# A cached-attention block on one core: new row sizes for K and V, one load queue, P as the weights of P*V, projection by token groups

## The chip, the cores and the metric

The kernel runs on one core of one Trainium2 chip. The time is the device time of one execution in microseconds. The profile is of one execution, and its span goes from the first to the last instruction.

## The reference

32 sequences (B) with 4 new tokens each attend to 2048 cached keys. There are 32 query heads in 4 groups (Hkv) of 8, a head has 128 columns, and all is bf16.

```python
q = (x @ wq).reshape(B, Sq, Hq, Dh).transpose(0, 2, 1, 3)      # x [32,4,1024], wq [1024,4096]
k = jnp.repeat(k_cache, rep, axis=1)                           # k_cache, v_cache [32,4,2048,128]
scores = jnp.einsum("bhqd,bhkd->bhqk", q, k) * (Dh ** -0.5)
p = softmax(scores, axis=-1)
o = jnp.einsum("bhqk,bhkd->bhqd", p, v)                        # v repeated like k
return o.transpose(0, 2, 1, 3).reshape(B, Sq, Hq * Dh) @ wo    # wo [4096,1024]
```

K and V are 67.1 MB each, wq and wo 8.4 MB each. One sequence ("a batch" below) has 2.1 MB of K and 2.1 MB of V, and its 32 heads by 4 tokens fill the 128 partitions of a score matrix of 128 by 2048, 32 partitions to a group.

## The kernel before

All instructions are written out by hand for each engine, with semaphores between them. The order on an engine is the order in the text.

- **Loads.** SP's queue has x, then wq in four parts of 1024 columns (line 278, rows of 2 KB), then K of batches 2 to 31, each as four loads of 512 KB, one for a group (line 283, rows of 4 KB); ACT's queue has K of batches 0 and 1 (L516). POOL's queue has V, one load of 2 MB per batch with rows of 4 KB (L268), and wo in 32 loads of 256 KB, one behind each V from batch 2 on (L260). K has two buffers, V three. K of batch b waits until K of b-2 has been transposed, V of b until P*V of b-3 is done.
- **K transposed.** PE turns K, 128 keys at a time, into a ring of four PSUM banks, eight transposes to a bank (a "fill", L312). DVE copies five of the eight fills of a batch to `KT_sb` (L444), ACT three (L446). This runs two batches ahead.
- **Scores.** 16 matmuls (L397) with the queries of one group as weights (32 columns) and 512 keys streaming, in four column tiles of PE, write `ps_s`, four banks. DVE takes the maximum over 2048 (L481) and scales it (L484), ACT takes the exponential with the row sum (L539) into `P_sb`.
- **P transposed and normalised.** DVE makes the reciprocal of the sum (L493) and a diagonal matrix of it (`diag`, L498). 16 matmuls of P with diag (L328) give the normalised transposed P in f32, four fills of the same ring; DVE and ACT copy two each to `PT_sb` (L444, L446).
- **P*V.** 64 matmuls (L346): a block of V, 128 by 128, is the weights and 32 columns of transposed P stream. The result is O transposed; DVE copies it to `oT_sb` (L453).
- **Projection.** After the last batch 64 matmuls of 512 columns (L418) with `oT_sb` as weights give the output for all 128 tokens; DVE and ACT copy a half each (L509, L556), and SP stores it (L286).

PE's order for batch i is QK of i, P*V of i-1, the fills of K of i+2, the transposes of P of i:

```python
for c in range(Sk // 512):
    for g in range(G):
        ins = eng.matmul(ps_s[32*g:32*(g+1), c*512:(c+1)*512], ...)   # QK of i
mark_ev("pe", ins, f"qk{i}")
if i >= 1:
    do_pv(i - 1)
if i + KT_AHEAD < B:
    do_kt_fills(i + KT_AHEAD)
do_tr_fills(i)
```

Of the kernel before, what the change touches and what calls it, by code (L numbers as in the profile page):

```python
# [12 lines left out]
class _Counter:  # L13

    def __init__(self, sem):
        self.sem = sem
        self.n = 0

    def mark(self, ins):
        self.n += 1  # L20
        ins.then_inc(self.sem, 1)
        return self.n


def bass_standalone__gqa_block_cached__sampling_kernel(
# [9 lines left out]
    _, Hkv, Sk, Dh = k_cache.shape  # L35
    Hq = wq.shape[1] // Dh
    REP = Hq // Hkv
    NT = B * Sq
    assert NT == 128 and Dh == 128 and Hkv * REP * Sq == 128 and D % 128 == 0
    assert Sk == 2048 and wo.shape[0] == Hq * Dh and wo.shape[1] == D and D == 1024  # L40
    KT = D // 128
    NKT = Sk // 128
    G = Hkv
    scale = float(Dh) ** -0.5
# [3 lines left out]
    NRING = 4  # L48
    KT_FILLS = 2 * G
    TR_FILLS = 4  # L50
    WQC = 1024
    NWQC = (Hq * Dh) // WQC
    HPC = WQC // Dh

# [3 lines left out]
    def kt_consumer(f):  # L58
        return "act" if f in (4, 6, 7) else "dve"

    def tr_consumer(f):
        return "dve" if f in (0, 2) else "act"

    jobs = []

    def add_kt(b):
        for f in range(KT_FILLS):
            jobs.append(("kt", b, f, kt_consumer(f)))

    def add_tr(b):  # L70
        for f in range(TR_FILLS):
            jobs.append(("tr", b, f, tr_consumer(f)))

    KT_AHEAD = 2
    for b in range(KT_AHEAD):
        add_kt(b)
    for i in range(B):
        if i + KT_AHEAD < B:
            add_kt(i + KT_AHEAD)
        add_tr(i)  # L80
    job_index = {(k, b, f): j for j, (k, b, f, c) in enumerate(jobs)}
    def last_pv_before_job(j):
        kind, b, f, _ = jobs[j]
        if kind == "kt":
            return b - KT_AHEAD - 1
        else:
            return b - 1

    ev = {}

    def plan():
        cnt = {"pe": 0, "dve": 0, "act": 0, "pool": 0}

        def mark(e, name):
            cnt[e] += 1
            assert name not in ev, name
            ev[name] = (e, cnt[e])

        mark("pool", "ident")
        mark("pe", "xT")  # L100
        for f in range(KT_FILLS):
            mark("pe", ("fill", job_index[("kt", 0, f)]))
        for j in range(Hq // 8):
            mark("pe", f"qproj_bank{j}")
        for f in range(KT_FILLS):
            mark("pe", ("fill", job_index[("kt", 1, f)]))
        for j in range(Hq // 8, Hq // 4):
            mark("pe", f"qproj_bank{j}")
        for i in range(B):
            mark("pe", f"qk{i}")  # L110
            if i >= 1:
                mark("pe", f"pv{i - 1}")
            if i + KT_AHEAD < B:
                for f in range(KT_FILLS):
                    mark("pe", ("fill", job_index[("kt", i + KT_AHEAD, f)]))
            for f in range(TR_FILLS):
                mark("pe", ("fill", job_index[("tr", i, f)]))
        mark("pe", f"pv{B - 1}")
        for c in range(2):
            mark("pe", f"oproj{c}")  # L120
        mark("dve", "xT_evac")
        for f in range(KT_FILLS):
            if kt_consumer(f) == "dve":
                mark("dve", ("evac", job_index[("kt", 0, f)]))
        for j in range(0, Hq // 8, 2):
            mark("dve", f"q_evac{j}")
        for f in range(KT_FILLS):
            if kt_consumer(f) == "dve":
                mark("dve", ("evac", job_index[("kt", 1, f)]))
        for j in range(Hq // 8, Hq // 4, 2):  # L130
            mark("dve", f"q_evac{j}")
        for i in range(B):
            mark("dve", f"max{i}")
            mark("dve", f"negmax{i}")
            if i >= 1:
                mark("dve", f"ot_evac{i - 1}")
            if i + KT_AHEAD < B:
                for f in (0, 1, 2):
                    if kt_consumer(f) == "dve":
                        mark("dve", ("evac", job_index[("kt", i + KT_AHEAD, f)]))  # L140
            mark("dve", f"rinv{i}")
            mark("dve", f"diag{i}")
            if i + KT_AHEAD < B:
                for f in range(3, KT_FILLS):
                    if kt_consumer(f) == "dve":
                        mark("dve", ("evac", job_index[("kt", i + KT_AHEAD, f)]))
            for f in range(TR_FILLS):
                if tr_consumer(f) == "dve":
                    mark("dve", ("evac", job_index[("tr", i, f)]))
        mark("dve", f"ot_evac{B - 1}")  # L150
        mark("dve", "out_evac0")
        for f in range(KT_FILLS):
            if kt_consumer(f) == "act":
                mark("act", ("evac", job_index[("kt", 0, f)]))
        for j in range(1, Hq // 8, 2):
            mark("act", f"q_evac{j}")
        for f in range(KT_FILLS):
            if kt_consumer(f) == "act":
                mark("act", ("evac", job_index[("kt", 1, f)]))
        for j in range(Hq // 8 + 1, Hq // 4, 2):  # L160
            mark("act", f"q_evac{j}")
        for i in range(B):
            mark("act", f"exp{i}")
            if i + KT_AHEAD < B:
                for f in range(KT_FILLS):
                    if kt_consumer(f) == "act":
                        mark("act", ("evac", job_index[("kt", i + KT_AHEAD, f)]))
            for f in range(TR_FILLS):
                if tr_consumer(f) == "act":
                    mark("act", ("evac", job_index[("tr", i, f)]))  # L170
        mark("act", "out_evac1")

    plan()

    with ExitStack() as es:
        w_sb = es.enter_context(nc.sbuf_tensor("w_sb", [128, KT, Hq * Dh], BF16))
        wq_sb = w_sb
        wo_view = w_sb[:, :, :].rearrange("p a (c n) -> p (a c) n", n=D)
        K_sb = es.enter_context(nc.sbuf_tensor("K_sb", [128, NKB, G, NKT * Dh], BF16))
        V_sb = es.enter_context(nc.sbuf_tensor("V_sb", [128, NVB, G, NKT * Dh], BF16))  # L180
        KT_sb = es.enter_context(nc.sbuf_tensor("KT_sb", [128, NKTB, G, Sk], BF16))
        QT_sb = es.enter_context(nc.sbuf_tensor("QT_sb", [128, B, Hq, Sq], BF16))
        oT_sb = es.enter_context(nc.sbuf_tensor("oT_sb", [128, Hq, NT], BF16))
        pp_sb = es.enter_context(nc.sbuf_tensor("pp_sb", [128, 2, Sk], BF16))
        P_sb = pp_sb[:, 0, :]
        PT_sb = pp_sb[:, 1, :].rearrange("p (t r) -> p t r", r=128)
        x_sb = pp_sb[:, 0, 0:D]
        xT_sb = pp_sb[:, 0, D:2 * D].rearrange("p (a b) -> p a b", b=128)
        out_sb = pp_sb[:, 1, 0:D]
        ident = es.enter_context(nc.sbuf_tensor("ident", [128, 128], BF16))  # L190
        diag = es.enter_context(nc.sbuf_tensor("diag", [128, 2, 128], BF16))
        mx = es.enter_context(nc.sbuf_tensor("mx", [128, B], F32))
        negmx = es.enter_context(nc.sbuf_tensor("negmx", [128, B], F32))
        ssum = es.enter_context(nc.sbuf_tensor("ssum", [128, B], F32))
        rinv = es.enter_context(nc.sbuf_tensor("rinv", [128, B], F32))

        ps_s = es.enter_context(nc.psum_tensor("ps_s", [128, Sk], F32))
        ps_a = es.enter_context(nc.psum_tensor("ps_a", [128, 512], F32))
        ps_b = es.enter_context(nc.psum_tensor("ps_b", [128, 512], F32))
        ps_c = es.enter_context(nc.psum_tensor("ps_c", [128, 512], F32))  # L200
        ps_o = es.enter_context(nc.psum_tensor("ps_o", [128, 512], F32))
        ring_f32 = [ps_a[:, :], ps_b[:, :], ps_c[:, :], ps_o[:, :]]
        ring_bf16 = [p.bitcast(BF16) for p in ring_f32]
        ps_x = ring_bf16[2]

        s_x = es.enter_context(nc.semaphore("s_x"))
        s_wq = [es.enter_context(nc.semaphore(f"s_wq{i}")) for i in range(NWQC)]
        s_wo = es.enter_context(nc.semaphore("s_wo"))
        s_out = es.enter_context(nc.semaphore("s_out"))
        s_k = [[es.enter_context(nc.semaphore(f"s_k{i}_{g}")) for g in range(G)] for i in range(NKB)]  # L210
        s_v = [es.enter_context(nc.semaphore(f"s_v{i}")) for i in range(NVB)]
# [376 lines left out]
```

## Time and profile before

| | us |
|---|---|
| the two runs shown | 411.44 and 409.82 |
| their median | 410.63 |
| span of the profiled execution (the page gives no other time of it) | 409.6 |
| PE, DVE, ACT busy | 306.7 (75%), 244.7 (60%), 197.2 (48%) |
| moved by DMA | 152.33 MB, mean 372 GB/s |

The page has the busy time of each engine, then the span in 40 slices of 10.2 us: a digit is the busy share in tenths, and GB/s is what the DMA engines moved. A group of instructions is shown with its line, engine, operation, the tile written and read, the count, busy time, mean duration in ns, idle time before it and what ended that. In the timeline the first column is the start, the second the duration. A row of waits has the total, the number of times and the longest.

### The profile page before, as it was taken

How to read it: one execution, taken by the hardware profiler on the slowest of the kernel's cores; microseconds unless marked ns; L12 is line 12 of the kernel's file. 1: busy time of each engine (PE TensorE's matmuls, PEld its weight loads, DVE VectorE, ACT ScalarE, POOL GpSimd, SP SyncE). 2: the span in 40 equal slices, each digit the busy share in tenths (PEclk: the TensorE clock that was granted, in tenths of full speed). 3: DMA queues.
4: the chain of work that ended last, by engine and by line, in shares of the span. 5: the costliest groups of instructions: out<-in, count | busy, mean ns of one | idle time of the engine just before them, and what ended most of it. 6: DMA issues, size and time to landing. Idle time of an engine off the chain costs nothing.

```text
span 409.6 us, 12650 instructions
## 1 busy us (share of the span) xinstructions
PE 306.7 (75%) x5448; PEld 251.4 (61%) x5448; DVE 244.7 (60%) x390; ACT 197.2 (48%) x230; POOL 42.0 (10%) x70
## 2 busy tenths in 40 slices
PE   4576877988777687577777777759876787775596
PEld 4476766867655576466666566548765676674442
DVE  2113286786666587677766776745875867765400
ACT  1213066474555555555555455553555555545300
POOL 0001011110100111111111111110110111120000
PEclk9799799998999899999999999997998989889679
DMA  8999999999999999999999999999999999997000
GB/s 307 400 387 401 408 408 407 407 406 407 407 407 408 405 406 407 406 407 407 408 404 407 407 407 406 407 407 406 407 406 407 407 407 408 403 402 308 38 2 26
DMA packets 42390, 152.33 MB, mean 372 GB/s; under 512 B 3168, under 2 KB 3168, under 8 KB 42336
## 3 DMA queue, kind: packets, MB, share of 16 engines
q0 software_dynamic: 19456, 75.50, 46.3%
q1 hardware_dynamic: 21728, 71.84, 44.7%
q10 hardware_dynamic: 1152, 4.19, 2.6%
q8 instruction: 44, 0.72, 0.7%
q14 instruction: 10, 0.08, 0.1%
HBM read 151.26 MB, written 0.26 MB: 370 GB/s over the span
## 4 chain that ended last, share of the span: by engine, by line
DMA 53%; PE 28%; issue 6%; SPq 5%; DVE 4%; ACT 3%; ACTq 0%; DVEq 0%
DMA K_sb<-in_k_cache_dram 32%; DMA V_sb<-in_v_cache_dram 15%; DMA w_sb<-in_wq_dram 6%; PE ps_o L346 5%; PE ps_s L418 4%; PE ps_o L312 4%; PE ps_s L397 3%; SPq L278 3%; PE ps_c L312 3%; PE ps_a L312 3%; PE ps_b L312 2%; SPq L283 2%; ACT KT_sb L446 2%; DVE mx L481 2%; PE ps_s L371 2%
## 5 line engine op out<-in xcount | busy, mean ns | idle before, releaser
L539 ACT ACTIVATE pp_sb<-ps_s,negmx 128x2048 bf16<-128x2048 f32 x32 | 62.9, 1967 | 98.7 <-DVE negmx L484 98.7
L481 DVE TENSOR_REDUCE mx<-ps_s 128x1 f32<-128x2048 f32 x32 | 73.3, 2292 | 43.8 <-PE ps_s L397 43.8
L346 PEld LDWEIGHTS ps_o<-pp_sb,V_sb 128*128 128x128 bf16 x2048 | 53.9, 96 | 25.9 <-issue 16.6
L346 PE MATMUL ps_o<-pp_sb,V_sb 128*128 128x32 bf16 x2048 | 57.4, 178 | 11.5 <-DMA V_sb<-in_v_cache_dram 7.0
L312 PE MATMUL ps_c<-ident,K_sb 128*128 128x128 bf16 x512 | 43.6, 232 | 19.7 <-DMA K_sb<-in_k_cache_dram 15.1
L268 POOL DMA_DIRECT2D V_sb<-in_v_cache_dram x32 | 23.8, 745 | 303.1 <-PE ps_o L346 274.4
L312 PE MATMUL ps_a<-ident,K_sb 128*128 128x128 bf16 x512 | 43.3, 232 | 13.7 <-issue 7.6
L444 DVE COPY KT_sb<-ps_b 128x1024 bf16<-128x1024 bf16 x64 | 43.7, 684 | 12.0 <-PE ps_b L312 11.9
L446 ACT ACTIVATE KT_sb<-ps_a 128x1024 bf16<-128x1024 bf16 x32 | 32.6, 1019 | 37.1 <-PE ps_a L312 37.0
L312 PE MATMUL ps_b<-ident,K_sb 128*128 128x128 bf16 x512 | 43.9, 233 | 7.9 <-issue 7.9
L312 PEld LDWEIGHTS ps_c<-ident,K_sb 128*128 128x128 bf16 x512 | 34.1, 105 | 21.6 <-DMA K_sb<-in_k_cache_dram 19.5
L312 PE MATMUL ps_o<-ident,K_sb 128*128 128x128 bf16 x512 | 43.1, 232 | 3.2 <-DVE KT_sb L444 3.1
L312 PEld LDWEIGHTS ps_a<-ident,K_sb 128*128 128x128 bf16 x512 | 32.9, 104 | 17.6 <-issue 12.0
L446 ACT ACTIVATE KT_sb<-ps_c 128x1024 bf16<-128x1024 bf16 x32 | 32.7, 1022 | 20.9 <-PE ps_c L312 20.9
L312 PEld LDWEIGHTS ps_b<-ident,K_sb 128*128 128x128 bf16 x512 | 34.7, 105 | 9.1 <-issue 8.5
L312 PEld LDWEIGHTS ps_o<-ident,K_sb 128*128 128x128 bf16 x512 | 34.2, 105 | 6.9 <-DVE KT_sb L444 4.4
L444 DVE CAST pp_sb<-ps_a 128x512 bf16<-128x512 f32 x32 | 22.1, 691 | 27.2 <-PE ps_a L328 27.2
L397 PE MATMUL ps_s<-KT_sb,QT_sb 128*32 128x512 bf16 x512 | 34.7, 391 | 2.6 <-ACT QT_sb L522 0.8
L446 ACT ACTIVATE KT_sb<-ps_o 128x1024 bf16<-128x1024 bf16 x32 | 32.7, 1023 | 0.0
L444 DVE COPY KT_sb<-ps_a 128x1024 bf16<-128x1024 bf16 x32 | 21.9, 685 | 10.2 <-PE ps_a L312 10.2
L371 PE MATMUL ps_s<-pp_sb,w_sb 128*128 128x128 bf16 x256 | 19.8, 255 | 10.0 <-DMA w_sb<-in_wq_dram 10.0
L371 PEld LDWEIGHTS ps_s<-pp_sb,w_sb 128*128 128x128 bf16 x256 | 19.2, 118 | 10.6 <-DMA w_sb<-in_wq_dram 10.6
(36 smaller groups left out, 288.9 us busy)
## 6 DMA issues: line engine op xcount, KB each, us to landing
V_sb<-in_v_cache_dram POOLq DMA_DIRECT2D x32, 2048.0 KB, 26.4
K_sb<-in_k_cache_dram SPq DMA_DIRECT2D x120, 512.0 KB, 14.6
w_sb<-in_wq_dram SPq DMA_DIRECT2D x4, 2048.0 KB, 25.2
w_sb<-in_wo_dram POOLq DMA_DIRECT2D x32, 256.0 KB, 26.1
K_sb<-in_k_cache_dram ACTq DMA_DIRECT2D x8, 512.0 KB, 10.7
pp_sb<-in_x_dram SPq DMA_DIRECT2D x1, 256.0 KB, 4.2
out_dram<-pp_sb SPq DMA_DIRECT2D x1, 256.0 KB, 2.0
```

The lines of the kernel that those rows point to most:

```text
L268: eng.dma_start(V_sb[:, vs, :, :], v_src(b)).then_inc(s_v[vs], 16)
L278: eng.dma_start(wq_sb[:, :, c * WQC:(c + 1) * WQC], wq_v[:, :, c * WQC:(c + 1) * WQC]).then_inc(s_wq[c], 16)
L283: eng.dma_start(K_sb[:, ks, g, :], k_src(b)[:, g, :]).then_inc(s_k[ks][g], 16)
L312: ins = eng.transpose(dst[:, q * 128:(q + 1) * 128], K_sb[:, ks, g, t * Dh:(t + 1) * Dh], ident[:, :],)
L346: ins = eng.matmul(ps_o[:, 32 * g:32 * (g + 1)], lhsT=V_sb[:, vs, g, t * Dh:(t + 1) * Dh], rhs=PT_sb[:, t, 32 * g:32 * (g + 1)], start=(t ...
L371: ins = eng.matmul(ps_s[:, col:col + 128], lhsT=wq_sb[:, kt, h * Dh:(h + 1) * Dh], rhs=xT_sb[:, kt, :], start=(kt == 0), stop=(kt == KT - 1),)
L397: ins = eng.matmul(ps_s[32 * g:32 * (g + 1), c * 512:(c + 1) * 512], lhsT=QT_sb[:, i, REP * g:REP * (g + 1), :], rhs=KT_sb[:, kts, g, c * ...
L418: ins = eng.matmul(ps_s[:, c * 512:(c + 1) * 512], lhsT=oT_sb[:, h, :], rhs=wo_view[:, h, c * 512:(c + 1) * 512], start=(h == 0), stop=(h ...
L444: ins = eng.tensor_copy(dst, src)
L446: ins = eng.activation(dst, src, ACT.Copy)
L481: ins = eng.tensor_reduce(mx[:, i:i + 1], ps_s[:, :], AX.X, ALU.max)
L539: ins = eng.activation(P_sb, ps_s[:, :], ACT.Exp, bias=negmx[:, i:i + 1], scale=scale, accum_out=ssum[:, i:i + 1],)
```

## The change

The kernel is written anew, with a list of operations for each engine that waits are worked out from.

- K of a batch is one load with rows of 16 KB: partition (g, r) holds 64 keys in a row. V keeps its rows of 4 KB, in which a partition holds 16 keys. wq is read in rows of 16 KB (two rows of wq to a partition and part), in four parts along the contraction. wo is four loads of 2 MB with rows of 2 KB. All loads are on SP's queue, in the order x, wq, K0, K1, V0, K2, then K and V by turns, and a part of wo behind V2 to V5. The last V is four loads, one for a group.
- A transpose of K now has the keys of all four groups in its columns. The copy to `KT_sb` sorts them: it reads PSUM at steps of 256 elements, four at a time, and writes in a row, so that the order of keys is that of V. Four fills of a batch are DVE's, four ACT's; the ring has three banks.
- P is transposed as it is (bf16, two fills, both copied by DVE). P*V has transposed P as its weights (32 columns) and V streaming (128 columns), in four column tiles; its result is O, which ACT multiplies by the reciprocal of the sum while copying it; PE transposes O, and ACT copies it to `oT_sb`. diag is gone.
- The projection is done for eight sequences (32 tokens) at a time, after batches 8, 16 and 24 and at the end: 128 matmuls of 256 columns in four column tiles. Four stores take each result out, on POOL's queue, at the end on SP's and ACT's.

The core of the diff (added lines; what is removed is in the functions above):

```diff
+        for c in range(4):
+            p.dma("sp", lambda e, c=c: e.dma_start(w_sb[:, 2 * c:2 * c + 2, :], wq_v[:, 2 * c:2 * c + 2, :]),
+                  [], ("wq", c), f"s_w{c}")
+        def load_k(b):
+            p.dma("sp", lambda e: e.dma_start(
+                K_sb[:, b % NKB, :, :], k_cache[b].rearrange("g (r t) d -> (g r) t d", r=R)),
+                [("fill", b - NKB, NFILL - 1)] if b >= NKB else [], ("k", b), f"s_k{b % NKB}")
+        def load_v(b):
+            src = v_cache[b].rearrange("g (p t) d -> p g (t d)", p=128)
...
+            waits = [("pv", b - NVB)] if b >= NVB else []
...
+        load_k(0)
+        load_k(1)
+        load_v(0)
+        load_k(2)
+        nk = 3
+        for b in range(1, B):
+            if nk < B:
+                load_k(nk)
+                nk += 1
+            load_v(b)
+            if b in (2, 3, 4, 5):
+                load_wo(b - 2)
...
+        def evac(b, f):
+            buf = slot_of["kt", b, f]
...
+            dst = KT_sb[:, b % NKTB, f * TB // C:(f + 1) * TB // C, :, :].rearrange("p v g (r c) -> p (v g) r c", c=C)
+            src = buf.rearrange("p (c m r) -> p m r c", c=C, r=R)
+            if f in DVE_FILLS:
+                p.op("dve", lambda e: e.tensor_copy(dst, src), waits, ("kt", b, f))
+            else:
+                p.op("act", lambda e: e.activation(dst, src, ACT.Copy), waits, ("kt", b, f))
...
+        def pv_mm(i, g, t, waits, done):
+            p.op("pe", lambda e: e.matmul(
+                ps_o[32 * g:32 * (g + 1), 0:Dh],
+                lhsT=PT_sb[:, t, 32 * g:32 * (g + 1)],
+                rhs=V_sb[:, i % NVB, g, t, :],
+                start=(t == 0), stop=(t == TV - 1), tile_position=(0, 32 * g)), waits, done)
...
+        def o_evac(i):
+            p.op("act", lambda e: e.activation(o_sb[:, :], ps_o[:, 0:Dh], ACT.Copy, scale=rinv[:, i:i + 1]),
+                 [("pv", i), ("rinv", i)] + ([("oT", i - 1)] if i else []), ("o", i))
...
+        def oproj(n):
...
+                        ps_o[32 * j:32 * (j + 1), 0:NC],
+                        lhsT=oT_sb[:, h, 32 * n:32 * (n + 1)],
+                        rhs=wo_sb[:, h, NC * j:NC * (j + 1)],
...
         for i in range(B):
+            pe_qk(i)
+            softmax_max(i)
             if i >= 1:
+                pe_pv(i - 1)
+                o_evac(i - 1)
+            if more:
+                for f in (0, 1):
+                    pe_fill(nb, f)
+                    evac(nb, f)
+            if i >= 1:
+                pe_ot(i - 1)
+                ot_evac(i - 1)
+            softmax_exp(i)
+            if more:
+                for f in range(2, NFILL):
+                    pe_fill(nb, f)
+                    evac(nb, f)
+            if i >= 1 and i % OG == 0:
+                oproj(i // OG - 1)
+                oproj_out(i // OG - 1)
+            softmax_rinv(i)
+            for f in range(2):
+                pe_pt(i, f)
+                evac_pt(i, f)
```

`nb` is i + 2. In it `pe_fill` is eight transposes of K into a bank of the ring, `evac` their copy, `pe_pt` eight transposes of P, `pe_ot` the transpose of O.

More of the change, by code (lines that the diff above doesn't have):

```diff
@@ L10, with __init__, op, dma @@
 F32 = mybir.dt.float32
[L13 to L22, printed above, removed]
+class _Program:
+    ENGINES = ("pe", "dve", "act", "pool", "sp")
+    def __init__(self):
+        self.ops = {e: [] for e in self.ENGINES}
+        self.count = {e: 0 for e in self.ENGINES}
+        self.at = {}
+        self.dma_count = {}
+    def op(self, engine, emit, waits=(), done=None):
+        if done is not None:
+            assert done not in self.at, done
+            self.count[engine] += 1
+            self.at[done] = (engine, self.count[engine])
+        self.ops[engine].append((emit, tuple(waits), done is not None, None))
+    def dma(self, engine, emit, waits, done, sem):
+        assert done not in self.at, done
+        self.dma_count[sem] = self.dma_count.get(sem, 0) + 16
+        self.at[done] = (sem, self.dma_count[sem])
+        self.ops[engine].append((emit, tuple(waits), False, sem))
+    def emit(self, name, engine, sems):
+        seen = {}
+        for emit, waits, counted, dma_sem in self.ops[name]:
+            need = {}
+            for w in waits:
+                s, n = self.at[w]
+                if seen.get(s, 0) < n:
+                    need[s] = max(need.get(s, 0), n)
+            for s, n in need.items():
+                engine.wait_ge(sems[s], n)
+                seen[s] = n
+            ins = emit(engine)
+            if counted:
+                ins.then_inc(sems[name], 1)
+            if dma_sem is not None:
+                ins.then_inc(sems[dma_sem], 16)
 def bass_standalone__gqa_block_cached__sampling_kernel(
@@ L109, in plan @@
         for i in range(B):
-            mark("pe", f"qk{i}")
+            nb = i + AHEAD
+            more = nb < B
+            pe_qk(i)
+            softmax_max(i)
             if i >= 1:
[L112 to L131, printed above, removed]
@@ L162, in plan @@
[L162 to L211, printed above, removed]
-        s_pe = es.enter_context(nc.semaphore("s_pe"))
-        s_dve = es.enter_context(nc.semaphore("s_dve"))
-        s_act = es.enter_context(nc.semaphore("s_act"))
-        s_pool = es.enter_context(nc.semaphore("s_pool"))
-        sems = {"pe": s_pe, "dve": s_dve, "act": s_act, "pool": s_pool}
-        counters = {k: _Counter(v) for k, v in sems.items()}
-        def wait_ev(eng, name):
-            e, n = ev[name]
-            eng.wait_ge(sems[e], n)
-        def mark_ev(e, ins, name):
-            n = counters[e].mark(ins)
-            assert ev[name] == (e, n), (name, ev[name], e, n)
@@ new lines, in bass_standalone__gqa_block_cached__sampling_kernel @@
+            softmax_rinv(i)
+            for f in range(2):
+                pe_pt(i, f)
+                evac_pt(i, f)
+        pe_pv(B - 1)
+        o_evac(B - 1)
+        pe_ot(B - 1)
+        ot_evac(B - 1)
+        oproj(NOG - 1)
+        oproj_out(NOG - 1)
+        names = list(p.ENGINES) + sorted({s for s in p.dma_count})
+        sems = {n: es.enter_context(nc.semaphore(f"e_{n}" if n in p.ENGINES else n)) for n in names}
+        p.op("sp", lambda e: None, [("out", n, j) for n in range(NOG) for j in range(4)])
@@ L411, in _ @@
-            do_pv(B - 1)
-            eng.wait_ge(s_wo, 16 * Hq)
-            wait_ev(eng, f"ot_evac{B - 1}")
-            wait_ev(eng, f"exp{B - 1}")
-            for c in range(2):
-                for h in range(Hq):
-                    ins = eng.matmul(
-                        ps_s[:, c * 512:(c + 1) * 512],
-                        lhsT=oT_sb[:, h, :],
-                        rhs=wo_view[:, h, c * 512:(c + 1) * 512],
-                        start=(h == 0),
-                        stop=(h == Hq - 1),
-                    )
-                mark_ev("pe", ins, f"oproj{c}")
@@ L512, in _ @@
+            p.emit("dve", eng, sems)
         @block.scalar
         def _(eng):
-            for b in range(KT_AHEAD):
-                for g in range(G):
-                    eng.dma_start(K_sb[:, b % NKB, g, :], k_src(b)[:, g, :]).then_inc(s_k[b % NKB][g], 16)
-            def act_q_evac(j):
-                bank = j % 4
-                wait_ev(eng, f"qproj_bank{j}")
-                src = ps_s[:, bank * 512:(bank + 1) * 512].rearrange("p (hh b s) -> p hh b s", hh=4, b=B, s=Sq)
-                dst = QT_sb[:, :, 4 * j:4 * j + 4, :].rearrange("p b hh s -> p hh b s")
-                ins = eng.activation(dst, src, ACT.Copy)
-                mark_ev("act", ins, f"q_evac{j}")
@@ L555, in _ @@
[L555 to L557 removed]
+            p.emit("act", eng, sems)
     return nc
```

546 lines of the change are left out of this document (185 added, 361 removed).

## The prediction

> **What bounds the kernel now.** I read the slices of the page first, then stretches of the windows view, then the chain that ended last.
>
> ```profile
> DMA  8999999999999999999999999999999999997000
> GB/s 307 400 387 401 408 408 407 407 406 407 407 407 408 405 406 407 406 407 407 408 404 407 407 407 406 407 407 406 407 406 407 407 407 408 403 402 308 38 2 26
> ...
> DMA 53%; PE 28%; issue 6%; SPq 5%; DVE 4%; ACT 3%; ACTq 0%; DVEq 0%
> ...
> out_dram<-pp_sb SPq DMA_DIRECT2D x1, 256.0 KB, 2.0
> ```
> ```profile
> 0.00:2.00 2.00, 0.00 (x0) 0.00 (x0) 0.00 (x0) 0.00 (x0) 0.69 (x6) 1.00 0.34 16
> 2.00:4.00 2.00, 0.00 (x0) 0.00 (x0) 0.00 (x0) 0.00 (x0) 0.00 (x0) 1.00 0.73 278
> ...
> 24.00:26.00 2.00, 0.00 (x0) 0.00 (x0) 0.00 (x0) 0.54 (x1) 0.00 (x0) 1.00 1.05 388
> 26.00:28.00 2.00, 1.92 (x35) 1.93 (x36) 0.00 (x0) 0.00 (x0) 0.00 (x0) 1.00 1.05 385
> 28.00:30.00 2.00, 2.00 (x40) 2.00 (x38) 0.69 (x1) 0.14 (x1) 0.00 (x0) 1.00 1.06 390
> ```
>
> The DMA engines are full from 4 us to about 370 us, at 407 GB/s, and the last 37 us move almost nothing. Before that, transfers set the pace (53% of the chain); after it, softmax of the last two batches and the projection. So a gain must come from fewer microseconds per byte or from a shorter end, and it lasts only while the engines keep up with the loads.
>
> How far are they from that? One batch that waited for no data, in the timeline:
>
> ```profile
> 284.62 1.05 PE L397 MATMUL ps_s<-KT_sb,QT_sb 128*32 128x512 bf16 x16
> ...
> 285.60 1.77 PE L346 MATMUL ps_o<-pp_sb,V_sb 128*128 128x32 bf16 x64
> ...
> 287.21 0.61 PE L312 MATMUL ps_a<-ident,K_sb 128*128 128x128 bf16 x8
> ...
> 287.66 0.61 PE L312 MATMUL ps_b<-ident,K_sb 128*128 128x128 bf16 x8
> ...
> 288.31 0.68 DVE L444 COPY KT_sb<-ps_a 128x1024 bf16<-128x1024 bf16 x1
> ...
> 288.91 0.68 DVE L444 COPY KT_sb<-ps_b 128x1024 bf16<-128x1024 bf16 x1
> ...
> 290.19 1.01 ACT L446 ACTIVATE KT_sb<-ps_a 128x1024 bf16<-128x1024 bf16 x1
> ...
> 291.09 1.02 ACT L446 ACTIVATE KT_sb<-ps_c 128x1024 bf16<-128x1024 bf16 x1
> ...
> 293.60 1.04 PE L397 MATMUL ps_s<-KT_sb,QT_sb 128*32 128x512 bf16 x16
> ```
>
> It runs from QK to QK in 8.98 us, and 4.19 MB of K and V at 407 GB/s take 10.3: 1.3 us to spare. The rows also give pitches: QK 0.98, PV 1.61, eight transposes 0.45 (ready 0.61 after their start), a contiguous DVE copy 0.60, an ACT copy 0.90. Part of the spare time is eaten by PE waiting for nothing shown, "issue":
>
> ```profile
> PE ps_b L312 <- issue: 7.9, 4, 2.6
> ...
> PE ps_a L312 <- issue: 7.6, 3, 2.9
> ...
> PE ps_o L346 <- issue: 3.6, 4, 1.6
> ...
> PE ps_c L312 <- issue: 2.5, 2, 2.0
> ```
> ```profile
> 270.55 1.05 PE L397 MATMUL ps_s<-KT_sb,QT_sb 128*32 128x512 bf16 x16 [0.19 <-ACT pp_sb L446]
> ...
> 276.36 0.69 PE L312 MATMUL ps_a<-ident,K_sb 128*128 128x128 bf16 x5 [2.88 <-issue]
> ```
>
> Thirteen such stalls, 21.6 us, 0.7 per batch. The batch with the 2.88 stall took 284.62 - 270.55 = 14.07.
>
> **The change: transfers.** The order on SP (load_k, load_v, load_wo) becomes x, wq, K0, K1, V0, K2, then K and V by turns, with four wo loads after V2 to V5. Bytes stay the same; K and wq go from 4 and 2 KB rows to 16 KB. Two row sizes are visible: at 24 to 30 us almost only wq moves (K0 and K1 were issued with the first of it, V starts at 30), 2 KB rows, 388 GB/s; later 4 KB, 407. For each of 16 engines that is 84.5 and 161.0 ns a row, so each further 2 KB adds 76.5 ns, and 16 KB would take 161.0 + 6 x 76.5 = 620 ns, 423 GB/s. Bounds: 407 (no gain) and 428 (the slope alone). I take 423. Until K31 has landed: start 2.6 us (the first two windows moved 0.59 MB by 4 us), x 0.7, wq 8.39 MB at 423 19.8, K 67.1 MB 158.7, V0 to V28 60.8 MB at 407 149.4, wo 8.39 MB at 388 21.6, and 1.4 of landing (the out row: 2.0 less 0.65 for its data). **K31 lands at 354.2.** A batch of loads takes 4.96 + 5.15 = 10.1 us.
>
> One queue in place of two: V and wo leave POOL and stand behind K on SP. K of batch b waits there for the last transposes of b-2, with V of b-2 queued behind it. When K of b-2 lands, three loads (15.3 us) are still queued and its transposes end 5.6 us later (below), so 9.7 us of cover is left; I cost the wait at nothing, and if the engines fall further behind, all of it shows. K now lands as one load of 2 MB; no group can be transposed when its quarter is there, as now. That shifts every batch by the same few microseconds, so it shows only at the end, where I count from the landing of all of K31. The stores of the first three token groups (four small ones each) stand alone on POOL and wait for nothing else.
>
> **The engines.** Per batch diag (254 ns) goes; the normalising moves to ACT; four P transposes with f32 results become two with bf16.
>
> ```profile
> L539 ACT ACTIVATE pp_sb<-ps_s,negmx 128x2048 bf16<-128x2048 f32 x32 | 62.9, 1967 | 98.7 <-DVE negmx L484 98.7
> L481 DVE TENSOR_REDUCE mx<-ps_s 128x1 f32<-128x2048 f32 x32 | 73.3, 2292 | 43.8 <-PE ps_s L397 43.8
> ...
> L444 DVE COPY KT_sb<-ps_b 128x1024 bf16<-128x1024 bf16 x64 | 43.7, 684 | 12.0 <-PE ps_b L312 11.9
> ...
> L444 DVE CAST pp_sb<-ps_a 128x512 bf16<-128x512 f32 x32 | 22.1, 691 | 27.2 <-PE ps_a L328 27.2
> ```
> ```profile
> L453 DVE CAST oT_sb<-ps_o 128x128 bf16<-128x128 f32 x32 | 9.1, 284 | 7.8 <-PE ps_o L346 7.7
> ```
>
> The costly edit is the K copy out of PSUM: it now reads four elements 512 bytes apart in turn. No row has such a read. At best it stays at 684 ns. DVE one element at a time costs (2292 - 691) / 1536 = 1.042 ns each (reduction against cast), so 691 + 512 x 1.042 = 1225 ns for 1024, pitch 1.14. At worst each element costs two such steps, the 2292 of the reduction. I take 1.14: the cast and the reduction are the nearest rows of a copy that takes no pairs. On ACT I keep pitch 0.90, with the same doubt upward.
>
> [...] Were 684 to stay, ACT's chain below would lead, pace 9.2, and the time would be 391 at the same stalls. No run here shows such a read yet.
>
> PV: again 64 pairs, but 128 columns stream past 32-column weights in four column tiles. QK runs in such tiles: 16 of 512 columns in 0.98, 61 ns each, where the transposes' 56 ns for 128 would make 224. So between 1.61 (the pairs' present pitch) and 64 x 56 ns = 3.6; I take 1.61, as four tiles at a time need under 1 us.
>
> The new batch, from QK: QK 0.98, PV to 2.59, two K fills to 3.49, one O transpose, the third fill ready at 4.2; DVE (max and negmx done at 3.6) copies fills 2, 3, 4, 6 at 1.14 until 8.8; the second P transpose waits for the buffer of fill 6, 8.9, and the next QK starts at **9.35**. ACT: O copy 0.28 (like L453), two K copies, O^T copy 0.28, exp at 5.2 to 7.2; the first P transpose waits for ACT's copy of fill 5 (8.2), so by ACT alone the next QK could start at 9.17: DVE covers it by 0.2 us only, and what ACT loses beyond that shows. Fill 7 ends 5.6 after fill 0. K must land by 2.6, else all after it shifts; exp now stands behind its first two copies on ACT too.
>
> 9.35 against 10.1 leaves 0.75. Three projections (oproj) go into the stream ahead of the P transposes: 128 pairs at 26.6 ns = 3.4 us each, 0.4 per batch over the 23 batches between wo and K31. Issue stalls: 0.7 before; fills that wait for copies anyway hide some, I take 0.5. Together 10.3, slightly over the pace: a **lag of 3 us** at the end (0 to 12 for stalls of 0 to 0.9).
>
> **The head** does not count: wq is first, 8.6 MB at 423 from 2.6 on, all there near 25 us; its last 64 pairs and the 16 fills of K0 and K1 at 1.14 for each two follow, the first QK is near 40, and then the wo loads hold K back for 21.6 us, in which the engines catch up.
>
> **The end.**
>
> ```profile
> 363.27 0.61 PE L312 MATMUL ps_a<-ident,K_sb 128*128 128x128 bf16 x8
> ...
> 370.66 1.05 PE L397 MATMUL ps_s<-KT_sb,QT_sb 128*32 128x512 bf16 x16
> ...
> 378.28 1.90 PE L397 MATMUL ps_s<-KT_sb,QT_sb 128*32 128x512 bf16 x16
> ...
> 388.14 1.87 PE L346 MATMUL ps_o<-pp_sb,V_sb 128*128 128x32 bf16 x64 [0.88 <-ACT pp_sb L446]
> ...
> 390.44 15.95 PE L418 MATMUL ps_s<-w_sb,oT_sb 128*128 128x512 bf16 x64 [0.43 <-issue]
> ...
> 394.58 11.32 PEld L418 LDWEIGHTS ps_s<-w_sb,oT_sb 128*128 128x128 bf16 x53 [0.19 <-issue]
> ...
> 406.43 0.60 ACT L556 ACTIVATE pp_sb<-ps_s 128x512 bf16<-128x512 f32 x1 [18.54 <-PE ps_s L418]
> ...
> 407.12 0.35 SPq L286 DMA_DIRECT2D out_dram<-pp_sb  x1
> ```
>
> From K31: fills to QK30 6.8 (9.35 - 2.59); QK30 to QK31 7.6 now, less rinv and diag 0.6, 7.0; QK31 to PV31 9.9 now, 9.1; PV 1.9; O copy, transpose, copy 1.2; the last token group's projection 5.5; y copy 0.5; out 2.5 + 0.4 for the second store of a queue. Sum 34.9, against 46 from K31's fills (363.27) now. The 5.5 come from the present projection: its first 4.2 us (390.4 to 394.6) hold 10 pairs, 420 ns each, the other 54 take 219 each, half of it, since PE had idled before. The new one should find PE the same: 79 of its 128 pairs at 53 ns, 49 at 26.6. V31 lands at 354.2 + 15.4 = 369.6, before PV31 wants it. 354.2 + 34.9 + 3 = 392.1 of span. The page's span is 409.6, the two runs 411.44 and 409.82, median 1.0 above it: **393 us**.
>
> **Rivals.**
> 1. *Strided reads cost more*, and DVE becomes the bound. It decides from a pace of 11.0 (354.2 - 23 x 10.1 = 121.9 for the first batch after wo; 121.9 + 23 x 11.0 + 35 + 1 = 411), that is K copies of 1.37 us in place of 1.22. At 1.76, midway between my value and the bound, 4 x 0.54 = 2.2 more a batch, pace 12.5: 445; at the bound about 510. For it: no row; ACT may suffer too. Against: casts and reductions read PSUM at one step. Chance 0.17. [...]
> 2. *The engines pace it for small reasons*: PV at 3.6, stalls as before, pace 10.6 to 11.3. 400 to 420, say 408. For it: 0.75 is little cover, less than the 1.3 now. Against: buffers absorb stalls. Chance 0.20.
> 3. *16 KB rows gain nothing*: K and wq at 407, 7 us more: 399. Chance 0.08.
> 4. *No lag and a warm end*: 380 to 388. Chance 0.05.
>
> **How the numbers follow.** The forecast has 0.50 (384 to 399). A run tells about 2% from no change: faster is under 402.4, slower over 418.8. Faster: 0.50, 0.05 of the fourth rival, 0.06 of the third, 0.02 of the second: 0.63. Slower: 0.15 of the first and 0.05 of the second: 0.20. Same: the remaining 0.17. The range, 383 to 428, takes in the second and third rival and the bounds of stalls, PV and rates; it leaves out the first beyond a pace of 11.7 (about 0.14) and a little below 383.
>
> **What would show it.** GB/s of 415 in late slices and K landing as one 2 MB load; DVE K copies near 1.22 us; QK to QK near 10.1 with waits on K for DMA; PV near 1.7; projection groups near 3.5; 35 us from K31's fills to the end. K copies over 1.4 us, PE waiting for DVE in fills, and DMA slices below 9 would show rival 1; the last but with copies at 1.2, rival 2.

## The result and the profile after

The changed kernel takes **398.1 us** (397.55 to 398.70, two runs) against 410.6: a ratio of 0.969, interval 0.962 to 0.975. The profiled execution took 398.7 us with a span of 396.9. The page of the changed kernel, its DMA slices, the queue that brings instructions (packets, MB, share of the engines' time), its chain and its DMA issues (KB each, then the median us from issue to landing):

```profile
DMA  8999999999999999999999999999999999999400
GB/s 330 433 423 418 390 408 395 414 409 396 413 412 418 416 418 409 422 415 419 414 414 417 416 417 387 424 414 417 417 418 416 419 400 391 418 418 404 165 0 9
...
q8 instruction: 46, 0.75, 0.8%
...
DMA 51%; DVE 23%; PE 21%; issue 2%; ACT 1%; SPq 1%
...
K_sb<-in_k_cache_dram SPq DMA_DIRECT2D x32, 2048.0 KB, 14.6
V_sb<-in_v_cache_dram SPq DMA_DIRECT2D x31, 2048.0 KB, 19.3
```

Two stretches of the windows view (after the five engines: granted clock, DMA share, GB/s):

```profile
20.00:25.00 5.00, 2.42 (x44) 2.25 (x42) 0.00 (x0) 0.00 (x0) 0.00 (x0) 1.00 1.02 433
...
150.00:200.00 50.00, 39.27 (x893) 30.63 (x883) 41.40 (x46) 30.44 (x39) 2.09 (x4) 1.00 1.02 416
```

As before, the DMA engines are full until K31 is there (9 tenths or more in every slice from the second on). While only wq and the first K moved they gave 433 GB/s (16 KB rows), and with V's 4 KB rows between them 416 (407 before). A few slices dip to 387 to 400. From 170 us on SP issues the loads of K 8.7 to 10.5 us apart, but 13.95 and 13.53 us apart where the projections at 231 and 313 us stand between them, and there the DMA engines are not full for a moment (a share of 0.71 below). The issues around the second one in the timeline (start, us), and a stretch of the windows:

```profile
313.57 0.34 SPq L137 DMA_DIRECT2D K_sb<-in_k_cache_dram  x1
327.10 0.34 SPq L137 DMA_DIRECT2D K_sb<-in_k_cache_dram  x1
```
```profile
326.00:328.00 2.00, 1.55 (x24) 1.32 (x24) 1.96 (x4) 1.81 (x3) 0.00 (x0) 1.00 0.71 285
```

The new operations, by groups of instructions (count, busy us, mean ns):

```profile
L228 DVE COPY KT_sb<-ps_r 128x1024 bf16<-128x1024 bf16 x128 | 147.7, 1216 | 53.1 <-PE ps_r L216 53.1
L230 ACT ACTIVATE KT_sb<-ps_r 128x1024 bf16<-128x1024 bf16 x128 | 127.9, 1026 | 67.6 <-PE ps_r L216 67.5
```

A batch that waited for no data, in the timeline, and then what PE waited for (us in total, times, longest):

```profile
328.13 1.05 PE L252 MATMUL ps_s<-KT_sb,QT_sb 128*32 128x512 bf16 x16
329.01 1.06 PE L260 MATMUL ps_r<-V_sb,PT_sb 128*32 128x128 bf16 x64
330.01 1.07 PE L216 MATMUL ps_r<-ident,K_sb 128*128 128x128 bf16 x16
...
336.85 1.05 PE L252 MATMUL ps_s<-KT_sb,QT_sb 128*32 128x512 bf16 x16
```
```profile
PE ps_r L216 <- DMA K_sb<-in_k_cache_dram: 44.1, 19, 6.0
...
PE ps_r L216 <- issue: 3.7, 3, 1.5
...
PE ps_r L260 <- issue: 1.0, 1, 1.0
```

QK to QK takes 8.72 us where nothing is late; PV's 64 pairs take 1.0 of it, 16 ns each. PE waits on K's transfer in 19 places, so the loads still seem to set the pace (the experiments test it), and the stalls for nothing shown are down from 21.6 us to 4.7.

The end of the chain that ended last (start, us, what):

```profile
359.35 1.05 PE ps_r L216 x16
...
366.24 1.01 PE ps_s L252 x16
...
373.78 1.61 PE ps_s L252 x12
...
382.71 5.68 PE ps_r L260 x61
...
389.44 3.71 PE ps_r L318 x128
393.17 0.42 DVE y_sb L326
```

The transposes of K31 start at 359.35 (before: 363.27), and 37.5 us follow (before: 46.3). Of the 12.7 us that the span lost, 3.9 were won ahead of K31 and 8.8 behind it.

### The profile page after: what moved, and what is told of

Read it like the earlier page. It is cut to its first block, busy times and chain, and to the rows that moved or that the text cites. A ratio compares the mean times of both kernels' runs of the same rounds, so it can differ in the third digit from the quotient of the medians.

```text
span 396.9 us, 12651 instructions
## 1 busy us (share of the span) xinstructions
PE 285.8 (72%) x5928; PEld 229.8 (58%) x5928; DVE 274.5 (69%) x297; ACT 207.7 (52%) x261; POOL 6.7 (2%) x18
## 4 chain that ended last, share of the span: by engine, by line
DMA 51%; DVE 23%; PE 21%; issue 2%; ACT 1%; SPq 1%
DMA K_sb<-in_k_cache_dram 51%; DVE KT_sb L228 18%; PE ps_r L216 9%; DVE mx L301 4%; PE ps_r L318 4%; PE ps_r L236 3%; PE ps_s L252 3%; PE ps_r L260 2%; ACT P_sb L306 1%; SPq L133 0%; DVE negmx L302 0%; PE ps_r L291 0%; DVE PT_sb L243 0%; DVE y_sb L326 0%; SPq L130 0%
## 5 line engine op out<-in xcount | busy, mean ns | idle before, releaser
L216 PE MATMUL ps_r<-ident,K_sb 128*128 128x128 bf16 x2048 | 150.5, 227 | 86.6 <-DMA K_sb<-in_k_cache_dram 44.1
L216 PEld LDWEIGHTS ps_r<-ident,K_sb 128*128 128x128 bf16 x2048 | 123.7, 101 | 112.4 <-issue 39.1
L228 DVE COPY KT_sb<-ps_r 128x1024 bf16<-128x1024 bf16 x128 | 147.7, 1216 | 53.1 <-PE ps_r L216 53.1
L230 ACT ACTIVATE KT_sb<-ps_r 128x1024 bf16<-128x1024 bf16 x128 | 127.9, 1026 | 67.6 <-PE ps_r L216 67.5
L301 DVE TENSOR_REDUCE mx<-ps_s 128x1 f32<-128x2048 f32 x32 | 73.3, 2292 | 10.1 <-PE ps_s L252 9.6
L306 ACT ACTIVATE P_sb<-ps_s,negmx 128x2048 bf16<-128x2048 f32 x32 | 63.4, 1980 | 1.3 <-DVE negmx L302 1.3
L287 ACT ACTIVATE o_sb<-ps_r,rinv 128x128 bf16<-128x128 f32 x32 | 11.8, 367 | 84.9 <-PE ps_r L260 84.9
L236 PE MATMUL ps_r<-ident,P_sb 128*128 128x128 bf16 x512 | 40.1, 226 | 6.6 <-ACT P_sb L306 6.2
L243 DVE COPY PT_sb<-ps_r 128x1024 bf16<-128x1024 bf16 x64 | 42.2, 690 | 3.1 <-PE ps_r L236 2.2
L260 PEld LDWEIGHTS ps_r<-V_sb,PT_sb 128*32 128x32 bf16 x2048 | 33.8, 98 | 12.1 <-DVE PT_sb L243 10.6
L260 PE MATMUL ps_r<-V_sb,PT_sb 128*32 128x128 bf16 x2048 | 38.9, 222 | 1.8 <-issue 1.0
L236 PEld LDWEIGHTS ps_r<-ident,P_sb 128*128 128x128 bf16 x512 | 30.4, 100 | 13.4 <-ACT P_sb L306 6.4
## 6 DMA issues: line engine op xcount, KB each, us to landing
K_sb<-in_k_cache_dram SPq DMA_DIRECT2D x32, 2048.0 KB, 14.6
V_sb<-in_v_cache_dram SPq DMA_DIRECT2D x31, 2048.0 KB, 19.3
V_sb<-in_v_cache_dram SPq DMA_DIRECT2D x4, 512.0 KB, 14.6
```

The source lines that it names most:

```text
L216: p.op("pe", lambda e, q=q, t=t: e.transpose(buf[:, q * 128:(q + 1) * 128], K_sb[:, b % NKB, t, :], ident[:, :]), waits + [("k", b), "iden ...
L228: p.op("dve", lambda e: e.tensor_copy(dst, src), waits, ("kt", b, f))
L230: p.op("act", lambda e: e.activation(dst, src, ACT.Copy), waits, ("kt", b, f))
L236: p.op("pe", lambda e, q=q: e.transpose(buf[:, q * 128:(q + 1) * 128], P_sb[:, (8 * f + q) * 128:(8 * f + q + 1) * 128], ident[:, :]), wai ...
L243: p.op("dve", lambda e: e.tensor_copy(PT_sb[:, 8 * f:8 * f + 8, :].rearrange("p t q -> p (t q)"), buf), waits, ("pt", i, f))
L260: p.op("pe", lambda e: e.matmul(ps_o[32 * g:32 * (g + 1), 0:Dh], lhsT=PT_sb[:, t, 32 * g:32 * (g + 1)], rhs=V_sb[:, i % NVB, g, t, :], sta ...
```

## Experiments

Each ratio is to the kernel before, on the same chip. There are three chips, on which that kernel took 409.9, 410.2 and 409.9 us, so times of different experiments are compared directly too.

### The changed kernel again

> The changed kernel as it is, for comparison with the others on this chip. Both theories: 398 us, 0.97 of the kernel before.

398.9 us (0.973, 0.970 to 0.977), span 397.8. Its median is the base of the times below. In its profile K31's transposes start at 360.53, in the first one at 359.35: a single profile fixes such a start to about 1.2 us.

### What the 16 KB rows of K are worth

```diff
-K_sb[:, b % NKB, :, :], k_cache[b].rearrange("g (r t) d -> (g r) t d", r=R)
+K_sb[:, b % NKB, :, :].rearrange("p (g t) d -> p g (t d)", g=G),
+k_cache[b].rearrange("g (p t) d -> p g (t d)", p=128)
```

> K comes by rows of 4 KB again, all else as changed (the keys then stand in another order than the copies out of PSUM sort them for, so the output is not the reference's; the work is the same). Theory A, the loads set the pace up to K31 and a chain of 37 us follows it: 67.1 MB at 407 in place of 426 GB/s is 7 us more, 405 us, K31 landing near 366 in place of 359, late slices near 407 GB/s. Theory B, the engines set the pace (DVE's strided copies and the maximum, 23% of the chain that ended last): no difference, 398 to 399.

405.0 us (0.988, 0.986 to 0.990). The GB/s slices of its page and K31 in its chain:

```profile
GB/s 332 428 407 378 385 389 399 407 399 398 405 396 409 409 408 407 410 409 407 408 409 407 407 408 396 403 407 408 408 409 407 408 410 389 408 407 408 236 0 9
```
```profile
366.28 1.05 PE ps_r L216 x16
```

Most late slices stand at 407 to 409, and K31's transposes start 6.9 us later than in the first profile, 5.8 later than in the second. K's long rows are worth 6.1 us of the time. Without them this kernel's K31 is later than that of the kernel before (363.27); why, no run here shows.

### K's copy out of PSUM in a row

```diff
-dst = KT_sb[...].rearrange("p v g (r c) -> p (v g) r c", c=C)
-src = buf.rearrange("p (c m r) -> p m r c", c=C, r=R)
+dst = KT_sb[...].rearrange("p v g q -> p (v g q)")
+src = buf
```

> The copy of K out of PSUM reads in a row and does not sort the keys (output not the reference's). DVE's copies fall from 1.22 to 0.69 us, 2.1 us less DVE per batch, and the free batch from 8.7 to about 8 us. Theory A: K31 lands at the same time within 3 us (the small holes in the loads after each projection close), the rest of the chain loses 0.5 to 1: 394 to 398. Theory B: DVE was the pace: 10 to 20 us less, 378 to 388.

397.9 us (0.970, 0.967 to 0.973): 1.0 less than the base, within the scatter of both. Its page, its waits, and a batch that waited for no data:

```profile
PE 286.2 (72%) x5928; PEld 238.0 (60%) x5928; DVE 215.1 (54%) x297; ACT 204.5 (52%) x261; POOL 6.7 (2%) x18
...
DMA 54%; PE 28%; ACT 12%; issue 2%; DVE 1%; SPq 1%
```
```profile
PE ps_r L216 <- DMA K_sb<-in_k_cache_dram: 51.1, 22, 7.1
PE ps_r L236 <- ACT KT_sb L230: 20.4, 26, 1.0
```
```profile
327.62 1.05 PE L252 MATMUL ps_s<-KT_sb,QT_sb 128*32 128x512 bf16 x16
...
336.31 1.05 PE L252 MATMUL ps_s<-KT_sb,QT_sb 128*32 128x512 bf16 x16
```

DVE fell from 274.5 to 215.1 us of work and from 23% to 1% of the chain. The free batch did not fall to 8 us as expected: it takes 8.69. PE's waits for DVE's copies (25.8 us) are gone, but the P transposes now wait for ACT's copies, up to 1.0 us in 26 batches, and ACT has 12% of the chain. So this run doesn't show what a shorter batch would bring. It shows that a share of the chain says where the path ran, not what can be won there: with DVE's copies short, ACT's stand in their place.

### The last P*V in tile order

```diff
-            if i < B - 1:
+            if True:     # t outer, g inner for the last batch too; V31 as one load
```

> The last P*V takes keys outermost and groups innermost like the others, with the last V as one load. Theory: its 5.7 us came from 16 pairs in a row in one column tile, which cannot run beside each other; in the new order it takes 1.1 to 1.9, the projection behind it may find PE at half clock (3.7 becomes 5): 2.5 to 4 us less, 394 to 396. Rival: it was slow from the halved clock alone, PE having idled before it: still above 3 us, 397 to 398.

396.0 us (0.966, 0.963 to 0.968), 2.8 less. In its chain,

```profile
381.88 1.93 PE ps_r L260 x44
...
384.91 6.44 PE ps_r L318 x117
```

and windows around the two operations, of this run, then of the changed kernel (the last three numbers: granted clock, DMA share, GB/s):

```profile
382.00:384.00 2.00, 1.78 (x64) 1.51 (x60) 0.00 (x0) 0.16 (x1) 0.00 (x0) 0.50 0.00 0
385.00:388.00 3.00, 3.00 (x60) 2.30 (x64) 0.00 (x0) 0.00 (x0) 0.00 (x0) 0.50 0.02 5
```
```profile
384.00:386.00 2.00, 2.00 (x30) 2.00 (x29) 0.00 (x0) 0.00 (x0) 0.00 (x0) 0.50 0.00 0
...
389.50:393.00 3.50, 3.50 (x128) 3.28 (x128) 0.00 (x0) 0.00 (x0) 0.00 (x0) 1.00 0.02 5
```

The last P*V takes 1.93 us in place of 5.68, both at half clock: 16 pairs in a row in one column tile cost 89 ns each, the same pairs 30 when the four tiles take turns. The projection behind it takes 6.44 in place of 3.71: after the long P*V it had the full clock (1.00 in the last row), after the short one half (0.50 in the second). So 2.7 of the 3.75 are given back; the rest of the 2.8 came ahead of P*V (it starts 0.8 sooner) or is scatter.

### V by 16 KB rows too

```diff
-src = v_cache[b].rearrange("g (p t) d -> p g (t d)", p=128)
+src = v_cache[b].rearrange("g (r t) d -> (g r) (t d)", r=R)
```

> V too comes by rows of 16 KB, a batch as one load (P*V then multiplies other keys' rows than the reference; the work is the same). Theory A, the row size sets the rate and the loads set the pace: V0 to V28 at 426 in place of 407 GB/s is 6.7 us less until K31 lands, 391 to 393 us, GB/s near 425 in late slices. Theory C, the engines are so close (8.7 free, some 9.6 with stalls and projections, against 9.85 of loads) that they take over: 394 to 397, PE's waits on K mostly gone.

V's tokens lie on other partitions then than the weights that they meet: its time is that of the transfers, and P*V is another sum. 391.4 us (0.953, 0.948 to 0.958).

```profile
GB/s 331 432 430 420 398 383 386 434 402 405 424 403 428 425 428 427 413 427 427 427 428 425 422 427 399 408 423 420 425 427 425 428 427 398 423 425 428 198 2 9
```
```profile
353.54 1.05 PE ps_r L216 x16
```

Most late slices are at 425 to 428, K31 is 5.8 us sooner than in the first profile, and the time is 7.5 lower: the loads set this kernel's time, and the rate went with the rows: 407 to 409 GB/s with K and V at 4 KB, 416 with K at 16 KB, 425 to 428 with both.

### One more copy of eight on DVE

```diff
-    ACT_FILLS = (0, 1, 5, 7)
-    DVE_FILLS = (2, 3, 4, 6)
+    ACT_FILLS = (0, 1, 5)
+    DVE_FILLS = (2, 3, 4, 6, 7)
```

> One more copy of K per batch goes from ACT to DVE, 1.16 us more on DVE's chain (five of eight). The free batch grows from 8.7 to 9.9, with projections and stalls some 10.7, past the 10.05 of the loads. Theory A with the cover of the prediction: the engines become the pace, 0.5 to 0.7 us for each of some 25 batches, 408 to 416 us. Rival, there is more cover than counted: 399 to 402.

404.2 us (0.984, 0.980 to 0.989), between the two. Its chain and its waits:

```profile
338.42 5.75 DVE KT_sb L228 x5
...
348.10 5.75 DVE KT_sb L228 x5
...
365.91 1.00 PE ps_r L216 x16
```
```profile
PE ps_r L216 <- DMA K_sb<-in_k_cache_dram: 19.4, 5, 5.2
```

Five copies in a row pace the batches at 9.68 us, and PE waits on K in 5 places only. That is still under the 10 us of a batch of loads, yet 5.3 us are lost. K31 has landed at 362.9, and its transposes start at 365.9: here is the lag of 3 us that the prediction had for the changed kernel. So the engines have little cover left; that projections and stalls come on top of the 9.68 is the likely reason.

### V on a queue of its own

```diff
-p.dma("sp", lambda e: e.dma_start(dst, src), waits, ("v", b), f"s_v{b % NVB}")
+p.dma("pool", lambda e: e.dma_start(dst, src), waits, ("v", b), f"s_v{b % NVB}")
 # V0 to V2 up front, V(i+2) behind P*V of batch i-1
```

> V goes back to POOL's queue (its loads stand there with the first twelve stores), K, wq and wo stay on SP's. Theory A, the number of queues does not matter to the rate: 397 to 401 us. Rival, one queue was part of the gain (no shared engines, or K ahead of V): 404 or more.

405.8 us (0.989, 0.984 to 0.994): a miss for theory A. Stretches of its windows, its issues, its chain:

```profile
170.00:180.00 10.00, 8.54 (x173) 6.28 (x169) 8.55 (x10) 6.36 (x8) 1.50 (x3) 0.93 0.73 267
190.00:340.00 150.00, 121.06 (x2687) 94.14 (x2684) 127.54 (x138) 95.81 (x122) 15.61 (x24) 1.00 1.02 417
```
```profile
K_sb<-in_k_cache_dram SPq DMA_DIRECT2D x32, 2048.0 KB, 11.8
V_sb<-in_v_cache_dram POOLq DMA_DIRECT2D x31, 2048.0 KB, 25.6
```
```profile
339.71 27.18 DMA V_sb<-in_v_cache_dram
```

The steady rate is the same, 417 GB/s. But K now overtakes V (11.8 us to landing against 25.6; 14.6 and 19.3 in one queue), there are holes in which neither queue had enough to move (267 GB/s around 175 us), and in the end the path waits for V28. This load has 16 landings in the records: eight came at 355.6 to 356.6, eight at 365.2 to 366.9 (V28 of the changed kernel: 349.1 to 353.9). So one queue doesn't raise the rate here (416). It hands the bytes over nearer the order of use (14.6 and 19.3 us to landing), and V28's parts lie closer together (4.8 us against 11.2); which of the two the 7 us are, this run doesn't separate.

### wo behind the last V

```diff
-            if b in (2, 3, 4, 5):
-                load_wo(b - 2)
+        for c in range(4):       # behind the last load_v
+            load_wo(c)
...
-            if i >= 1 and i % OG == 0:
-                oproj(i // OG - 1)
-                oproj_out(i // OG - 1)
...
-        oproj(NOG - 1)
-        oproj_out(NOG - 1)
+        oproj_all()              # all 128 tokens at once, 64 pairs of 512 columns, by wo's four parts
```

> The last P*V in tile order as before, wo loaded after the last V, and the projection done once at the end for all 128 tokens, 512 columns at a time in the order in which wo's four parts land (not by token groups). Theory A: K31 lands 21.6 us sooner, near 338, its chain of 30 us to the last O ends near 368 while V29 to V31 and wo land until 375; then 16 pairs, a copy and a store: 381 to 386 us. Rival, the engines cannot follow without the pause that the wo loads gave them in batches 2 to 6: K31 near 348 or later, 390 to 396.

The last P*V is in tile order and V31 one load here too, worth 2.8 us by themselves. **382.8 us** (0.933, 0.929 to 0.938): faster than both kernels. Its page and timeline:

```profile
GB/s 331 436 422 418 391 417 420 417 412 416 415 416 414 415 416 416 418 417 419 418 416 418 417 411 415 422 413 417 411 419 394 416 416 418 417 406 397 386 292 53
```
```profile
336.53 1.05 PE L216 MATMUL ps_r<-ident,K_sb 128*128 128x128 bf16 x16 [1.27 <-DMA K_sb<-in_k_cache_dram]
...
373.75 3.63 PE L316 MATMUL ps_s<-w_sb,oT_sb 128*128 128x512 bf16 x16 [0.27 <-DMA w_sb<-in_wo_dram]
```

K31 is there 22.8 us sooner than in the first profile. wo's 8.39 MB at 388 GB/s are 21.6 of them (an estimate; the windows of the last run below have 388 and 387 from 340 to 360 us, where mostly wo moves); the rest is within what a profile can tell, and may be the dips, most of which are gone with the three projections. wo moves while the last two batches are computed. wo's last quarter is now what ends last, at 373.75.

### The loads behind K31 held back

By now one question was open: the rates were as predicted, and still K31 was complete 5 us late.

```diff
             waits = [("pv", b - NVB)] if b >= NVB else []
+            if b == B - 3:
+                waits.append(("k", B - 1))
```

> V29 waits on SP until K31 has landed, so V29, V30 and V31 (6.3 MB) can no longer move ahead of K31's last bytes; the rest is unchanged. Theory A (the loads queued behind K31 move about 2.4 MB before K31 is complete, 5.8 us at 415 GB/s): K31 lands near 354 instead of 359, V29 is there near 361 and V31 near 371, both before their P*V wants them, and the time falls to 393 to 395. Rival (K31 is late because the loads ahead of it are slow, and the order within the queue is kept): K31 lands at 358 to 360 as before, DMA idles for about 2 us, V31 lands near 376, and the time is 398 to 402.

398.5 us (0.972, 0.969 to 0.976), no change: theory A falls. Windows of this run (in the changed kernel 428 and 389 GB/s in the first two), and K31 in its timeline:

```profile
354.00:356.00 2.00, 1.74 (x28) 1.41 (x32) 1.96 (x4) 1.75 (x2) 0.00 (x0) 1.00 0.50 205
356.00:358.00 2.00, 1.88 (x81) 1.19 (x80) 1.70 (x3) 0.07 (x1) 0.00 (x0) 1.00 0.35 147
358.00:360.00 2.00, 0.96 (x18) 0.99 (x19) 1.48 (x2) 0.61 (x2) 0.00 (x0) 1.00 0.04 12
```
```profile
359.04 1.05 PE L218 MATMUL ps_r<-ident,K_sb 128*128 128x128 bf16 x16 [1.16 <-DMA K_sb<-in_k_cache_dram]
```

The rival's times hold, but its reason only half: the engines don't stop together after K31. From 354 on half of their time is idle, and the last finish near 359. Nothing stood behind K31 to move ahead of it, and still its last bytes came no sooner (359.04 against 359.35 and 360.53). The landing records say the same. The 16 parts of K31, in us before the last one:

```
changed kernel   -5.2 -5.1 -5.0 -5.0 -5.0 -4.9 -4.9 -4.7 -1.9 -1.5 -1.3 -1.0 -1.0 -0.9 -0.3 0.0
V29 held back    -4.6 -4.6 -4.5 -4.5 -4.5 -4.4 -4.4 -4.3 -2.1 -1.1 -1.0 -1.0 -0.4 -0.3 -0.1 0.0
V on POOL        -1.8 -1.8 -1.8 -1.8 -1.7 -1.7 -1.7 -1.7 -1.7 -1.6 -1.6 -1.6 -1.6 -1.6 -0.7 0.0
```

Eight parts came at about 354.3, eight over the last 2 us. The lag is larger later in the run: the last part of K0 stands 1.7 us behind its eighth, that of K16 about 3, that of K31 4.7. It doesn't come of K's long rows (from first to last part of K31 5.3 us with 4 KB rows) nor of the projections (6.6 with wo behind the last V). With five copies on DVE, where the loads are less of a bound, it is 2.6. With V on POOL it is small for K31, but V28's is the 11.2 us seen above. In the changed kernel K31's 16 parts land up to 5.2 us apart, and its transposes start only behind the last (359.21 and 359.35); the prediction had not used it.

### Both savings together

wo behind the last V, and V by 16 KB rows, with the same change to the last P*V as above. As with V's rows alone, the time is that of the transfers, and P*V is another sum.

> Two changes that each gained, together: wo behind the last V with one projection at the end, and V by 16 KB rows. If they add up (V's rows gave 7.5 us, wo's place 16): K31 lands near 330, the last part of wo near 367, late slices near 426 GB/s, and the time is 374 to 377. If the engines take over the pace once loads cost 9.8 us a batch (the free batch is 8.7, and stalls come to it), K31 lands later than 333 and PE waits on K in fewer than 15 places: 378 to 383.

377.6 us (0.921, 0.918 to 0.925), just above the upper end for "they add up". In its timeline:

```profile
330.72 1.05 PE L216 MATMUL ps_r<-ident,K_sb 128*128 128x128 bf16 x16 [1.02 <-DMA K_sb<-in_k_cache_dram]
...
357.21 15.34 PE L316 MATMUL ps_s<-w_sb,oT_sb 128*128 128x512 bf16 x64 [0.46 <-ACT oT_sb L293]
```

K31 comes 5.8 us sooner, as with V's rows alone. PE still waits on K in 28 places, so the engines don't pace it. But wo is no longer late: the end is now the projection's own 15.3 us, and only 5.2 of the 7.5 us arrive.

## Why the prediction was right, and where it was off

The forecast was 393 us, 17.6 less than before; 398.1 is 12.5 less. It lies inside the range, and nearest of all to the third rival's 399, whose reason is refuted: 16 KB rows gained what was predicted. That the number came so close is in part luck, since errors of 5 and 3 us had opposite signs. Step by step, on the profiled execution:

- **Rates**: 423 GB/s for 16 KB rows beside 407 for 4 KB ones gives 415 for the mix. Measured 433 (wq and K alone, early), 425 to 428 (late, with V's rows at 16 KB too) and 416 for the mix. Right; K at 4 KB cost 6.1 us, where the prediction has 7 for K and wq.
- **K31 lands at 354.2**: its first eight parts did, its last one at 359.2, and the transposes start at 359.35, 5.1 late. Here the step failed, in the term "1.4 of landing". The mean of the 16 parts lies 3.0 us before the last (from the list above), at 356.2. So 3.0 of the 5.1 us are spread among the parts, and some 2 are bytes that moved late on the average. The sum left out two things that can make them, and no run separates these. It counts loads alone, but the page has 0.75 MB of instructions as well, and 0.20 MB of the stores of the first three token groups; some 0.9 MB of that moved before K31 was there, 2.2 us at 416 GB/s (an estimate). And there are the dips behind the projections at 231 and 313. At 244 to 248 us the windows have 336 and 352 GB/s, at 326 to 330 285 and 344; against 416 that is 0.7 and 1.0 us (an estimate). A rate slightly above the predicted 415 elsewhere gives part of both back.
- **One queue, wait of SP at nothing**: nearly right, as late slices are full but for these two dips, in which the wait shows: a load of K waits for the transposes of two batches before, and the projection (3.68 us on PE) holds those up. With wo at the end and no projection in the stream, most dips are gone; the projections were not tried by themselves. That two queues would do as well was only implied, and V on POOL cost 7 us.
- **Strided copy**: 1216 ns against 1225, and ACT's 1026 against 1019 to 1023 before. Rival 1 falls. The 1225 was the author's estimate from a cast and a reduction (691 and 2292 ns), and the time bears it out; how DVE takes the elements, no run shows. A copy in a row still took 690 (P's, in the changed kernel). That DVE has little cover is shown from one side: a fifth copy cost 5.3 us. The other side, short copies, left the batch at 8.69 because ACT's copies end it then; the prediction had ACT only 0.2 behind DVE.
- **PV at 1.61**: 1.03. The bound given from below was too high: 64 pairs in four column tiles took 1.03 us, 16 ns a pair. With it the free batch is 8.72 instead of 9.35. Stalls are 4.7 us in the whole run instead of 0.5 in each batch. So the **lag of 3 us** is none: the transposes of K31 start when it lands. Rival 2 falls with it.
- **The end, 34.9 from K31**: 37.5. K31's fills to QK30 6.9 (6.8), QK30 to QK31 7.5 (7.0), QK31 to PV31 8.9 (9.1), then **PV31 5.7 instead of 1.9**, the projection 3.7 instead of 5.5. The prediction took the last P*V like the others, although its loop goes by groups: one column tile for 16 pairs. And it took PE into the projection as at half clock, which only the run in tile order shows (6.44, at a granted clock of 0.50 up to 388 us; in the changed kernel it was 1.00, and 29 ns a pair where the prediction has 26.6). The store took 3.3 instead of 2.9.
- **Around the span**: 1.8 instead of 1.0 us in the profiled execution.
- **Sums of the rivals**: three don't come out of their own terms. A pace of 11.0 needs copies of 1.40 us and not 1.37, the bound of 2.29 gives some 490 us and not 510, and 7 us more than 393 are 400. The forecast rests on none of them.

Together: 393.1, +5.1 (K31), -3 (lag), +2.6 (end), +0.8 (around) = 398.6, against 398.7.

So the mechanism held: long rows make the loads shorter (6.1 us for K's), one queue keeps their order, the engines fit beside them, the end is shorter. What stays open is why half of the parts of a load come late, and later as the run goes on; no run here took that apart.

## What to carry to other kernels

K31 was there when its slowest part was there, 3.0 us behind the mean of its 16 parts, so look at the spread of the landings and not at GB/s alone. Count all bytes of the stretch, instructions and stores too (some 0.9 MB here). When loads pace a kernel, first ask which bytes the last chain doesn't need: moving wo behind the last V, with one projection at the end and the last P*V in tile order, brought 16 us, more than the whole change. And the last P*V, cheap where four column tiles take turns (1.93 us), was not cheap in another loop order (5.68, both at half clock).

## What was not expected of the hardware

- P*V with 32-column weights in four column tiles: 16 ns a pair of 128 columns when the tiles take turns (1.0 us for 64), 30 at half clock (0.50 granted), but 89 at half clock when one tile takes 16 pairs in a row.
- A copy out of PSUM whose source hops 512 bytes takes DVE 1216 ns for 1024 elements, against 684 in a row in the kernel before; ACT takes 1026, against 1019 to 1023.
- The last of the 16 parts of a 2 MB load comes 1.7 us behind the eighth at K0 and 4.7 at K31. With V on a queue of its own, K31's parts lay within 1.8, but V28's within 11.2.
